# Retention units of 256 tokens and 4 heads in 512-byte rows on 64 by 64 tiles, with the whole program in a searched order

## The chip, the cores and the metric

One core of one Trainium2 chip. The metric is device microseconds of one execution. A change of less than 2% counts as the same. A run over 1.5% above the fastest of its kernel is called slow and left out of the ratios. In the kernel text, tiles in PSUM take the results of matmuls; `dma_start_transpose` (a DMA transpose) copies a tile and swaps its rows and columns on the way, which `nc.tensor.transpose` does on TensorE.

## The reference, cut to what matters

```python
batch, n_heads, seq, head_dim = (4, 8, 768, 64)          # float32 throughout
# part 1: retention, for every batch and head
for t in range(S):
    state = gamma * state + k[t] (x) v[t]                # 64 x 64 outer product
    x[t]  = scale * q[t] @ state
# part 2, for every batch, d_model = 512
theta = x @ w_theta
zr, zi = x * cos(theta), x * sin(theta)
y = w_tok_r @ zr + w_tok_i @ zi                          # 768 x 768, over tokens
u = x + y
out = u + relu(u @ w_ch)
```

## The kernel before

Tokens are cut into 24 chunks of 128 with all 8 heads. Decay is put into q and v by exponents (`qsc`, `vsc`), so a chunk is scores, outputs and a state sum. The parts that the change touches:

```python
def load_chunk(n):                       # q, k, v: 256 KB each, rows of 64 floats
    for name, src in (("kf", k), ("qf", q), ("vf", v)):
        t = io.tile([P, H, D], FT, name=name, bufs=9)
        nc.sync.dma_start(out=t, in_=src[b, :, c * P:(c + 1) * P, :].rearrange("h s d -> s h d"))
...
N_DMA = (B - 1) * nT + 1                 # chunks from here on: k, q and x transposed by DMA
M_DMA = (B - 2) * nT                     # output tiles from here on: u transposed by DMA
...
def att_A(n):                            # scores: 4 x 2 matmuls, 64 rows by 128 columns
    for j in range(NP):
        for par in range(2):
            rows = slice(par * D, (par + 1) * D)
            nc.tensor.matmul(at_ps[:, par, j, :], kqT[rows, j, :], kqT[rows, NP + j, :], ...)
...
def att_Y(n):                            # outputs, then the state sum, which stays in PSUM
    ...
    for j in range(NP):
        nc.tensor.matmul(st_ps[b][:, j, :], s["kb"][:, j * P:(j + 1) * P],
                         s["vb"][:, j * P:(j + 1) * P], start=(c == 0 and j == 0), ...)
...
for s_ in range(last_slot):              # the order: one loop over slots
    if n is not None and n + 5 < NCH and n >= nT + 2:
        load_chunk(n + 5)
    ...
```

All loads, stores and DMA transposes stand on one queue, SyncE's, in program order. With `N_DMA` = 19 and `M_DMA` = 12 the DMA transposes (5 of k and q, 5 of x, 11 of u) come when the loads are nearly done. GpSimd makes all bf16 copies of k, q and v; VectorE makes all products z.

Of the kernel before, what the change touches and what calls it, by code (L numbers as in the profile page):

```python
# [14 lines left out]
FT = mybir.dt.float32  # L15
# [3 lines left out]
PSUM = bass.MemoryType.PSUM  # L19

# [12 lines left out]
def kernel(  # L33
# [13 lines left out]




# [6 lines left out]
    NP = H // 2  # L57
    scale = 1.0 / math.sqrt(D)
    gammas = [1.0 - 2.0 ** (-5.0 - h) for h in range(H)]
    NCH = B * nT  # L60

    N_DMA = (B - 1) * nT + 1
    M_DMA = (B - 2) * nT
# [8 lines left out]


    raw = {}

    def load_chunk(n):
        b, c = divmod(n, nT)
        for name, src in (("kf", k), ("qf", q), ("vf", v)):
            t = io.tile([P, H, D], FT, name=name, bufs=9)
            nc.sync.dma_start(  # L80
                out=t, in_=src[b, :, c * P:(c + 1) * P, :].rearrange("h s d -> s h d"))
            raw[n, name] = t

    wdma = {}

    def load_w512(name, src):
        t = io.tile([P, nD, dm], FT, name="w512", bufs=2)
        nc.sync.dma_start(out=t, in_=src.rearrange("(a p) e -> p a e", p=P))
        wdma[name] = t

    def load_wtok(r, t0):
        src = (moe_w_tok_r, moe_w_tok_i)[r]
        t = io.tile([P, S], FT, name="wtok", bufs=4)
        nc.sync.dma_start(out=t, in_=src[t0 * P:(t0 + 1) * P, :])  # L94
        wdma[r, t0] = t

    for what in ("c0 c1 th c2 c3 c4 w0 c5 w1 w2 c6 w3 c7 ch c8 w4 c9 c10 w5 c11 "
                 "c12").split():
        if what == "th":
            load_w512("th", moe_w_theta)  # L100
        elif what == "ch":
            load_w512("ch", moe_w_ch)
        elif what[0] == "c":
            load_chunk(int(what[1:]))
        else:
            for r in range(2):
                load_wtok(r, int(what[1:]))


    posn = const.tile([P, nT], FT)  # L110
    nc.gpsimd.iota(posn, pattern=[[P, nT]], base=1, channel_multiplier=1,
                   allow_small_or_imprecise_dtypes=True)
    lg = const.tile([P, H], FT)
    for h in range(H):
        nc.gpsimd.memset(lg[:, h:h + 1], math.log(gammas[h]))
    lscale = const.tile([P, 1], FT)
    nc.gpsimd.memset(lscale, math.log(scale))
    halfpi = const.tile([P, 1], FT)
    nc.gpsimd.memset(halfpi, math.pi / 2.0)
    zerob = const.tile([P, 1], FT)  # L120
    nc.gpsimd.memset(zerob, 0.0)
    arg = const.tile([P, nT, H], FT)
    nc.vector.tensor_mul(arg, _bcast_last(posn, H), _bcast_mid(lg, nT))
    vsc = const.tile([P, nT, H], FT)
    nc.scalar.activation(vsc, arg, AF.Exp, bias=zerob, scale=-1.0)
    qsc = const.tile([P, nT, H], FT)
    nc.scalar.activation(qsc, arg, AF.Exp, bias=lscale, scale=1.0)
    ident = const.tile([P, P], BF)
    make_identity(nc, ident)
    mask = const.tile([P, P], BF)  # L130
    nc.gpsimd.memset(mask, 1.0)
    nc.gpsimd.affine_select(out=mask, in_=mask, compare_op=ALU.is_ge, fill=0.0,
                            base=0, pattern=[[1, P]], channel_multiplier=-1)
    stbd = []
    for i in range(2):
        t = const.tile([P, NP, P], BF, name=f"stbd{i}")
        nc.vector.memset(t, 0.0)
        stbd.append(t)

    wth = const.tile([P, nD, dm], BF)  # L140
    wch = const.tile([P, nD, dm], BF)
    wT = [const.tile([P, nT, S], BF, name="wtr"), const.tile([P, nT, S], BF, name="wti")]
# [4 lines left out]
    def att_prep(n):  # L147
        c = n % nT
        r3 = "p (h d) -> p h d"
        kqb = work.tile([P, 2, dm], BF, name="kqb", bufs=5)  # L150
        kb, qb = kqb[:, 0, :], kqb[:, 1, :]
        vb = work.tile([P, dm], BF, name="vb", bufs=5)
        nc.gpsimd.tensor_copy(kb.rearrange(r3, h=H), raw[n, "kf"])  # L153
        nc.gpsimd.tensor_mul(qb.rearrange(r3, h=H), raw[n, "qf"],  # L154
                             _bcast_last(qsc[:, c], D))
        nc.gpsimd.tensor_mul(vb.rearrange(r3, h=H), raw[n, "vf"],  # L156
                             _bcast_last(vsc[:, c], D))
        st[n] = dict(kqb=kqb, kb=kb, qb=qb, vb=vb)

    def att_T(n):  # L160
        s = st[n]
        kq_ps = psum.tile([P, 2 * NP, P], BF, name="kq_ps", tag="tr", bufs=2)
        for i, src in enumerate((s["kb"], s["qb"])):
            for j in range(NP):
                nc.tensor.transpose(kq_ps[:, i * NP + j, :],  # L165
                                    src[:, j * P:(j + 1) * P], ident)
        kqT = work.tile([P, 2 * NP, P], BF, name="kqT", bufs=4)
        nc.vector.tensor_copy(kqT, kq_ps)  # L168
        s["kqT"] = kqT

    def att_T_dma(n):
        s = st[n]
        kqT = work.tile([P, 2 * NP, P], BF, name="kqT", bufs=4)
        nc.sync.dma_start_transpose(
            out=kqT, in_=s["kqb"].rearrange("p a d -> p (a d)"))
        s["kqT"] = kqT

    def att_A(n):
        s = st[n]
        kqT = s["kqT"]  # L180
        at_ps = psum.tile([P, 2, NP, P], FT, name="at_ps", tag="at", bufs=1)
        for j in range(NP):
            for par in range(2):
                rows = slice(par * D, (par + 1) * D)
                nc.tensor.matmul(at_ps[:, par, j, :], kqT[rows, j, :],  # L185
                                 kqT[rows, NP + j, :], start=(j == 0),
                                 stop=(j == NP - 1), skip_group_check=True)
        at = work.tile([P, 2, NP, P], BF, name="at", bufs=2)
        nc.vector.tensor_mul(at.rearrange("p a j t -> p (a j) t"),  # L189
                             at_ps.rearrange("p a j t -> p (a j) t"),  # L190
                             _bcast_mid(mask, H))
        s["at"] = at

    st_ps = {}
    xs, zs = {}, {}

    def att_Yinter(n):
        c = n % nT
        s = st[n]
        s["yT_ps"] = psum.tile([P, NP, P], FT, name="yT_ps", tag="acc", bufs=2)  # L200
        if c > 0:
            for j in range(NP):
                nc.tensor.matmul(s["yT_ps"][:, j, :], stbd[c % 2][:, j, :],  # L203
                                 s["kqT"][:, NP + j, :], start=(j == 0), stop=False,
                                 skip_group_check=True)

    def att_Y(n):
        b, c = divmod(n, nT)
        s = st[n]
        yT_ps = s["yT_ps"]  # L210
        for j in range(NP):
            for par in range(2):
                h = 2 * j + par
                nc.tensor.matmul(yT_ps[par * D:(par + 1) * D, j, :],  # L214
                                 s["vb"][:, h * D:(h + 1) * D], s["at"][:, par, j, :],
                                 start=(c == 0 and j == 0), stop=(j == NP - 1),
                                 skip_group_check=True)
        if c < nT - 1:
            if c == 0:
                st_ps[b] = psum.tile([P, NP, P], FT, name="st_ps", tag="st", bufs=1)  # L220
            for j in range(NP):
                nc.tensor.matmul(st_ps[b][:, j, :], s["kb"][:, j * P:(j + 1) * P],  # L222
                                 s["vb"][:, j * P:(j + 1) * P],
                                 start=(c == 0 and j == 0),
                                 stop=(c == nT - 2 and j == NP - 1),
                                 skip_group_check=True)
        if c == 0:
            xs[b] = big.tile([P, nT, dm], BF, name="x_sb")
            zs[b] = big.tile([P, nT, 2, dm], BF, name="z")
        xT = work.tile([P, NP, P], BF, name="xT", bufs=3)  # L230
        nc.scalar.copy(xT, yT_ps)  # L231
        s["xT"] = xT
        if c < nT - 1:
            for par in range(2):
                sl = slice(par * D, (par + 1) * D)
                nc.scalar.copy(stbd[(c + 1) % 2][sl, :, sl], st_ps[b][sl, :, sl])  # L236

    def att_X_dma(n):
        b, c = divmod(n, nT)
        nc.sync.dma_start_transpose(  # L240
            out=xs[b][:, c, :].rearrange("p (j e) -> p j e", j=NP),
            in_=st[n]["xT"].rearrange("p j t -> p (j t)"))

    def att_X(n):
        b, c = divmod(n, nT)
        s = st[n]
        if n < N_DMA:
            x_ps = psum.tile([P, NP, P], BF, name="x_ps", tag="tr", bufs=2)
            for j in range(NP):
                nc.tensor.transpose(x_ps[:, j, :], s["xT"][:, j, :], ident)  # L250
# [267 lines left out]
```

## Time and profile before

| | before |
|---|---|
| time, median of the first 3 runs | 185.08 us (183.41 to 185.79) |
| profiled span | 181.8 us, granted clock 0.994 |
| TensorE idle in all (trace) | 20.2 us |
| DMA transposes | 21 |
| time from 60 to 118 us below 100 GB/s | 1.2 us |

The page's lines on the engines, the packets and the chain of waits:

```profile
PE 157.7 (87%) x1367; PEld 90.7 (50%) x1392; DVE 104.8 (58%) x146; ACT 74.7 (41%) x140; POOL 79.9 (44%) x104
DMA packets 95265, 35.63 MB, mean 196 GB/s; under 512 B 89488, under 2 KB 89744, under 8 KB 95248
PE 62%; SPq 18%; DMA 12%; issue 2%; POOL 2%; DVE 1%; DVEq 0%
```

The reader is to see that TensorE makes up 62% of the chain that ended last, that nearly all packets are under 512 bytes, and that VectorE has a lot of room (58%).

### The profile page before, as it was taken

How to read it: one execution, taken by the hardware profiler on the slowest of the kernel's cores; microseconds unless marked ns; L12 is line 12 of the kernel's file. 1: busy time of each engine (PE TensorE's matmuls, PEld its weight loads, DVE VectorE, ACT ScalarE, POOL GpSimd, SP SyncE). 2: the span in 40 equal slices, each digit the busy share in tenths (PEclk: the TensorE clock that was granted, in tenths of full speed). 3: DMA queues.
4: the chain of work that ended last, by engine and by line, in shares of the span. 5: the costliest groups of instructions: out<-in, count | busy, mean ns of one | idle time of the engine just before them, and what ended most of it. 6: DMA issues, size and time to landing. Idle time of an engine off the chain costs nothing.

```text
span 181.8 us, 3528 instructions
## 1 busy us (share of the span) xinstructions
PE 157.7 (87%) x1367; PEld 90.7 (50%) x1392; DVE 104.8 (58%) x146; ACT 74.7 (41%) x140; POOL 79.9 (44%) x104
## 2 busy tenths in 40 slices
PE   0567987897764999999999999999999999999991
PEld 0344655553542655656565565455545544444560
DVE  1264794716822777878676877765645744434442
ACT  4053764821429535647554363356345332200010
POOL 4648677869075768865777847250000000000000
PEclk9999999999999999999999999999999999999997
DMA  6999999999998999999999989984483333334433
GB/s 128 222 316 218 224 276 259 294 288 231 227 259 180 260 243 225 222 272 271 223 228 251 266 208 233 263 151 115 119 112 102 103 97 90 104 93 110 132 105 117
DMA packets 95265, 35.63 MB, mean 196 GB/s; under 512 B 89488, under 2 KB 89744, under 8 KB 95248
## 3 DMA queue, kind: packets, MB, share of 16 engines
q1 hardware_dynamic: 95104, 35.27, 86.4%
q8 instruction: 11, 0.18, 0.5%
q10 hardware_dynamic: 144, 0.13, 0.2%
q14 instruction: 6, 0.05, 0.1%
HBM read 25.69 MB, written 6.29 MB: 176 GB/s over the span
## 4 chain that ended last, share of the span: by engine, by line
PE 62%; SPq 18%; DMA 12%; issue 2%; POOL 2%; DVE 1%; DVEq 0%
PE y_ps L282 27%; SPq L80 15%; PE o_ps L310 11%; PE th_ps L253 8%; DMA kf<-in_k_dram 4%; DMA qf<-in_q_dram 3%; PE yT_ps L214 3%; DMA wtok<-in_moe_w_tok_r_dram 3%; PE at_ps L185 3%; PE kq_ps L165 3%; PE st_ps L222 2%; SPq L94 2%; DMA uT<-u 2%; PE yT_ps L203 2%; PE x_ps L250 1%
## 5 line engine op out<-in xcount | busy, mean ns | idle before, releaser
L282 PE MATMUL y_ps<-z,wti 128*128 128x512 bf16 x137 | 51.9, 379 | 1.6 <-ACT wti L332 0.9
L282 PE MATMUL y_ps<-z,wtr 128*128 128x512 bf16 x125 | 47.4, 379 | 0.7 <-DVE u L287 0.3
L189 DVE TENSOR_TENSOR at<-at_ps,mask 128x1024 bf16<-128x1024 f32 x24 | 29.3, 1220 | 8.9 <-PE at_ps L185 8.8
L258 ACT ACTIVATE cs<-th_ps,halfpi 128x512 bf16<-128x512 f32 x24 | 16.5, 688 | 38.0 <-PE th_ps L253 34.1
L154 POOL TENSOR_TENSOR kqb<-qf,qsc 128x512 bf16<-128x512 f32 x24 | 25.7, 1071 | 11.3 <-DMA qf<-in_q_dram 11.1
L156 POOL TENSOR_TENSOR vb<-vf,vsc 128x512 bf16<-128x512 f32 x24 | 25.9, 1081 | 7.0 <-DMA vf<-in_v_dram 5.8
L264 DVE TENSOR_TENSOR z<-cs,x_sb 128x1024 bf16<-128x1024 bf16 x24 | 19.6, 818 | 14.2 <-ACT cs L259 14.2
L168 DVE COPY kqT<-kq_ps 128x1024 bf16<-128x1024 bf16 x19 | 13.1, 691 | 24.6 <-PE kq_ps L165 24.4
L253 PE MATMUL th_ps<-wth,xT 128*128 128x512 bf16 x89 | 24.4, 387 | 2.4 <-DVE wth L395 1.9
L153 POOL CAST kqb<-kf 128x512 bf16<-128x512 f32 x24 | 16.0, 667 | 19.9 <-DMA kf<-in_k_dram 14.1
L310 PE MATMUL o_ps<-wch,uT 128*128 128x512 bf16 x88 | 23.1, 379 | 0.4 <-DMA uT<-u 0.2
L165 PE MATMUL kq_ps<-ident,kqb 128*128 128x128 bf16 x152 | 13.6, 234 | 11.1 <-POOL kqb L153 7.0
L287 DVE TENSOR_TENSOR u<-y_ps,x_sb 128x512 bf16<-128x512 f32 x23 | 15.8, 690 | 11.9 <-PE y_ps L282 11.9
L313 DVE SCALAR_TENSOR_TENSOR ot<-o_ps,u 128x512 f32<-128x512 f32 x23 | 15.9, 692 | 10.7 <-PE o_ps L310 10.7
L231 ACT CAST xT<-yT_ps 128x512 bf16<-128x512 f32 x24 | 14.1, 586 | 19.4 <-PE yT_ps L214 18.1
L282 PEld LDWEIGHTS <-wti 128*128 128x128 bf16 x138 | 13.5, 98 | 15.4 <-issue 1.9
L282 PEld LDWEIGHTS <-wtr 128*128 128x128 bf16 x138 | 13.5, 98 | 13.5
L165 PEld LDWEIGHTS <-kqb 128*128 128x128 bf16 x152 | 10.6, 104 | 16.5 <-POOL kqb L153 7.9
L259 ACT ACTIVATE cs<-th_ps,zerob 128x512 bf16<-128x512 f32 x24 | 16.3, 681 | 0.0
L236 ACT CAST stbd<-st_ps 64x256 bf16<-64x256 f32 x40 | 14.7, 366 | 0.5
L310 PEld LDWEIGHTS <-uT 128*128 128x128 bf16 x92 | 8.8, 98 | 10.3 <-DMA uT<-u 0.4
L253 PEld LDWEIGHTS <-xT 128*128 128x128 bf16 x96 | 8.8, 100 | 9.2 <-issue 2.6
(51 smaller groups left out, 147.3 us busy)
## 6 DMA issues: line engine op xcount, KB each, us to landing
kf<-in_k_dram SPq DMA_DIRECT2D x24, 256.0 KB, 4.9
qf<-in_q_dram SPq DMA_DIRECT2D x24, 256.0 KB, 5.0
vf<-in_v_dram SPq DMA_DIRECT2D x24, 256.0 KB, 5.3
out_dram<-ot SPq DMA_DIRECT2D x23, 256.0 KB, 2.2
wtok<-in_moe_w_tok_r_dram SPq DMA_DIRECT2D x6, 384.0 KB, 5.3
wtok<-in_moe_w_tok_i_dram SPq DMA_DIRECT2D x6, 384.0 KB, 5.9
w<-in_moe_w_theta_dram SPq DMA_DIRECT2D x1, 1024.0 KB, 6.7
w<-in_moe_w_ch_dram SPq DMA_DIRECT2D x1, 1024.0 KB, 7.8
```

Of the source, the lines that this page charges most:

```text
L80: nc.sync.dma_start(out=t, in_=src[b, :, c * P:(c + 1) * P, :].rearrange("h s d -> s h d"))
L153: nc.gpsimd.tensor_copy(kb.rearrange(r3, h=H), raw[n, "kf"])
L154: nc.gpsimd.tensor_mul(qb.rearrange(r3, h=H), raw[n, "qf"], _bcast_last(qsc[:, c], D))
L156: nc.gpsimd.tensor_mul(vb.rearrange(r3, h=H), raw[n, "vf"], _bcast_last(vsc[:, c], D))
L165: nc.tensor.transpose(kq_ps[:, i * NP + j, :], src[:, j * P:(j + 1) * P], ident)
L189: nc.vector.tensor_mul(at.rearrange("p a j t -> p (a j) t"), at_ps.rearrange("p a j t -> p (a j) t"), _bcast_mid(mask, H))
L253: nc.tensor.matmul(th_ps, s["xT"][:, j, :], wth[:, j, :], start=(j == 0), stop=(j == NP - 1))
L258: nc.scalar.activation(cs[:, 0, :], th_ps, AF.Sin, bias=halfpi, scale=1.0)
L259: nc.scalar.activation(cs[:, 1, :], th_ps, AF.Sin, bias=zerob, scale=1.0)
L264: nc.vector.tensor_mul(zs[b][:, c], st[n]["cs"], _bcast_mid(xs[b][:, c, :], 2))
L282: nc.tensor.matmul(y_ps, wT[r][:, s0, t0 * P:(t0 + 1) * P], zs[b][:, s0, r, :], start=(s0 == 0 and r == 0), stop=(s0 == nT - 1 and r == 1))
L310: nc.tensor.matmul(o_ps, mo[m]["uT"][:, j, :], wch[:, j, :], start=(j == 0), stop=(j == nD - 1))
```

## The change

Its intent: make the loads cheaper (rows of two tokens, 512 bytes), pack the small attention matmuls as 64 by 64 tiles, make one visit to the attention shapes per unit instead of three, and put every instruction where a search found it best. The core of the diff:

```diff
+ORDER = """
+Lk.0 Lq.0 Lv.0 Lk.1 const1 const2 Lq.1 const4 const6 Lth const3 const5 Lv.1 ck.0.p warm.8 Tk.0
+... (852 tokens in all: operation, unit or tile, engine; D* is a DMA transpose, T* one on TensorE)
+M.7.1 M.7.2 SU.13 XA.12.1 Dk.16 M.7.3 z.10.v SB.13.0.a SB.13.1.p Du.5 I.13 G.14 z.11.v M.7.4
+...
-    def load_chunk(n):
-        ...
-                out=t, in_=src[b, :, c * P:(c + 1) * P, :].rearrange("h s d -> s h d"))
+    def load_unit(name, src, n):
+        b, i, h = unit(n)                       # 256 tokens, 4 heads
+        t = io.tile([P, HU, 2, D], FT, name=name, bufs=9)
+        nc.sync.dma_start(
+            out=t.rearrange("p h a d -> p h (a d)"),
+            in_=src[b, h * HU:(h + 1) * HU, i * 2 * P:(i + 1) * 2 * P, :].rearrange(
+                "h (p a) d -> p h (a d)", a=2))
 ...
+    def A(n):                                   # 16 matmuls of 64 x 64 x 128; Y(n), ST(n) alike
+                        nc.tensor.matmul(at_ps[cols, g, j, a, :],
+                                         kqT[rows, 0, a, j, cols], kqT[rows, 1, :, j, cols], ...)
 ...
+    def SU(n):                                  # state sums: float32 in SBUF, added by VectorE
+            nc.vector.tensor_add(s2[i % 2][:, 1], ds[0], s2[i % 2][:, 0])
+        if i < nI - 1:
+            nc.vector.tensor_add(s2[(i + 1) % 2][:, 0], ds[1], s2[i % 2][:, 1])
 ...
+    def z(C, e):                                # the engine is given by the order:
+        engines[e].tensor_mul(st["z", b][:, c], st["cs", C], _bcast_mid(x_of(C), 2))
```

DMA transposes rise from 21 to 49.

## The prediction

> **What bounds the kernel now.** I read the page's slices first, then the sums by stretch, the DMA rates of the first stretch, the chain of waits, and a few microseconds of the timeline at full density. The slices show two regimes:
>
> ```profile
> PE   0567987897764999999999999999999999999991
> DMA  6999999999998999999999989984483333334433
> ```
>
> DMA is full for the first 26 slices (118 us); TensorE is full only from slice 13 (59 us) on. By stretch (TensorE, weight load, VectorE, ScalarE, GpSimd, granted clock, DMA share and GB/s):
>
> ```profile
> 0.00:59.00 59.00, 40.50 (x415) 25.16 (x422) 29.79 (x42) 27.02 (x50) 37.66 (x60) 1.00 1.06 240
> 59.00:118.00 59.00, 57.96 (x563) 34.94 (x573) 44.21 (x60) 29.38 (x56) 39.65 (x42) 1.00 1.13 244
> 118.00:172.00 54.00, 53.63 (x354) 26.82 (x360) 27.21 (x38) 17.52 (x34) 2.62 (x3) 1.00 0.47 109
> ```
>
> So the first 59 us are set by loads, the next 59 by TensorE with DMA just as full, the last 64 by TensorE alone. The chain of waits agrees: before 59 us it is nearly all queue issue and landings, after it nearly all matmuls.
>
> ```profile
> 42.13 7.52 DMA kf<-in_k_dram
> ...
> 51.51 6.18 DMA qf<-in_q_dram
> ...
> 83.46 0.33 PE at_ps L185 x8
> 83.79 0.34 PE yT_ps L214 x8
> 84.13 0.33 PE st_ps L222 x4
> ```
>
> How fast do loads go? The DMA rates of 2 to 20 us, in 40 slices:
>
> ```profile
> GB/s 108 239 282 275 245 205 227 224 222 214 212 223 222 219 220 245 245 382 382 391 396 370 286 274 221 217 217 218 218 214 218 220 216 218 218 219 218 216 219 217
> ```
>
> The right half is q, k and v alone, in rows of 64 floats (256 bytes): 218 GB/s, flat, 1.20 us per 256 KB load. The hump of about 385 is the theta weight, in 2048-byte rows. The row length sets the rate.
>
> What does TensorE cost when it is full? One chunk (start, duration; a matmul's duration includes its drain, so I take differences of starts):
>
> ```profile
> 82.86 0.38 PE L282 MATMUL y_ps<-z,wtr 128*128 128x512 bf16 x1
> 83.08 0.38 PE L282 MATMUL y_ps<-z,wti 128*128 128x512 bf16 x1
> 83.39 0.40 PE L185 MATMUL at_ps<-kqT 64*128 64x128 bf16 x8
> 83.72 0.41 PE L214 MATMUL yT_ps<-at,vb 128*64 128x128 bf16 x8
> 84.06 0.40 PE L222 MATMUL st_ps<-vb,kqb 128*128 128x128 bf16 x4
> 84.30 0.39 PE L250 MATMUL x_ps<-ident,xT 128*128 128x128 bf16 x4
> 84.52 1.03 PE L253 MATMUL th_ps<-wth,xT 128*128 128x512 bf16 x4
> ```
>
> A 512-column matmul takes 0.216 us. Four of 128 columns take 0.22 (x_ps). The attention trio takes 84.30 - (83.08 + 0.216) = 1.00 us, of which 0.66 is columns and about 0.1 at each of three changes of tile shape.
>
> **What the Trainium skill says.** "DMA: Bandwidth & Descriptors", sections Specifications and "Why small descriptors are slow (HBM only)", puts line rate at 512 bytes and up and gives 256-byte descriptors 11 cycles where 8 move data. The trace agrees on the direction (218 against 385 GB/s); nothing here has run at 512. "TensorEngine Tiling (Array Packing)", Key Properties, says changing the tiling mode drains TensorE while tiles of one mode run independently; the trace agrees (the 0.1 us before at_ps; eight 128-column matmuls of half size in the 0.22 that four whole ones take). Its Restrictions say column tiling turns off fast weight load; yT_ps, column tiled already, still keeps the pace. "SBUF — State Buffer", Who interferes with whom, says VectorE and GpSimd lock a shared port; z took 0.70 us usually and 1.34 beside GpSimd work at 25 us, which agrees.
>
> **The change part by part.** (1) Loads. 72 loads of 256 KB keep their bytes but use 512-byte rows. Per engine and packet, 256 bytes at 218 GB/s is 18.8 ns and 2048 at 385 is 85 ns; a straight line gives 28.3 ns for 512, so 290 GB/s and 0.90 us a load (estimate). Saved: 72 x 0.30 = 21.6 us of DMA time.
>
> (2) More transposes go to DMA: 17 of k and q against 5 (1024 packets of 256 bytes each, 1.2 us), 14 of x and 18 of u against 5 and 11 (0.6 us each): 39.6 against 15.6 us, adding 24.0. So the DMA total does not fall: before 72 x 1.20 + 15.6 + theta and channel weights 5.4 + token rows 12 x 0.98 + stores 24 x 0.68 = 135 us; after 65 + 40 + 5 + 12 + 16 = 138.
>
> (3) TensorE. Before: 480 matmuls of 512 columns, 103.7; trio 24 x 1.00 less four missing state sums, 23; k and q transposes 19 x 0.45 = 8.5; x 19 x 0.22 = 4.3; inter-chunk 20 x 0.22 = 4.5; u 2.9; token weights 4.0. Sum 151. After: the big ones as they are, 103.7; k and q 7 x 0.45 = 3.1; x 10 x 0.22 = 2.2; u 1.3; token weights 4.0; inter-chunk 16 x 0.22 + 8 x 0.11 = 4.4. The trio becomes one visit of 48 matmuls on 64 by 64 tiles, four at once: scores and outputs four rounds of 0.055 each, 0.22 + 0.22, state sums (64 columns) 0.11 to 0.22, and two changes of shape for three, 0.2: 0.75 to 0.87, take 0.8, x 24 = 19. Sum 138. Saved: 13 us.
>
> (4) State. The sum leaves PSUM for a float32 copy in SBUF: 40 small VectorE adds and 48 half-block casts on three engines. I put VectorE at 115 to 120 us for 105, GpSimd and ScalarE at 70 to 80. None bounds. PSUM pays: the transpose and accumulator pools lose their second buffer, and one y buffer must be read (0.69) before the next product starts, which the order fills with other matmuls.
>
> (5) Order. The end of a program in which DMA is full early and TensorE full late is at least (DMA time up to some transfer) + (TensorE work from its user on). Going through the order, the transfers that give the most sit late. One of them is the transpose of u of tile 11: ahead of it and with it on the one queue are 66 loads 59.7, the two wide weights 5.4, 12 token rows 11.8, 14 k/q transposes 16.8, 14 x and u transposes 8.4, 8 stores 5.4: 107.5 us. First bytes move at 2 us and a transpose lands 1.8 after its packets: 111. From its product on: 62 pairs of y matmuls 26.8, 14 outputs 12.1, 6 theta 5.2, 5 visits 4.0, 5 inter-chunk 1.1, the halved last tile 3.7: 53. Before, the last matmul ended 3.8 us ahead of the span's end. 111 + 53 + 4 = 168 with a DMA that never idles. Early transfers give less: the first six units (18 loads 16.3, theta 2.7) leave about 125 behind them, so about 150. TensorE alone gives 138 + 10 of start + 4 = 152.
>
> **Sum.** Span 168 by the DMA path, 2 to 4 more for DMA idling at waits of the queue, less what a 512-byte packet may be better than my line: 165 as the span. Timed runs stand 3.3 us over the profiled span now (185.1 and 181.8), so 168 as the time. The gain of 17 us is mostly TensorE time taken away (13) and an earlier start; DMA stays full to about 120 us.
>
> **The rivals.** (a) 512 bytes is nearly line rate: 0.75 us a load, 10 us less ahead of tile 11. For it: the skill's threshold; against it: 2048 bytes still cost a fixed part per packet. The time would be 159 to 162, with TensorE the bound again. (b) Small tiles do not run four at once (weights, or issue of 96 instructions in 0.6 us): a visit takes 1.4 instead of 0.8, 14 us more TensorE work, though part lies under full DMA. Against it: pairs start together in both directions now. Time 175 to 182. (c) The queue is the bound: a transpose holds it 1.2 us when idle and 2 to 4 when loaded; 49 of them with waits on VectorE and TensorE ahead of loads. For it: first-stretch pieces in which the queue waits for GpSimd. Time 173 to 178. (d) Single PSUM buffers stall TensorE 0.5 us a tile, 24 times: 12 us, mostly hidden under DMA up to 110 us, 4 or 5 after. Time 172.
>
> **Range and chances.** (a) pulls to 160, (b) to (d) to 178; each alone is a minor chance, and to stay within 2% (above 181.4) two of the bad ones must come together. Predicted 168, range 160 to 178. Faster 0.93, same 0.05, slower 0.02.
>
> **What would show it.** Load landings 0.90 us apart and 285 to 295 GB/s in the opening; TensorE lost time before it fills falling from 26 us (59 less the 33 of the 151 done by then) to about 20, spread rather than at the start; DMA full to about 115 us; visits of 0.75 to 0.87 us start to start; TensorE waits named on kqT, uT or x_sb from DMA. I am wrong if visits exceed 1.0 us, if loads come at 1.1 us or more, or if TensorE waits mostly for VectorE or ScalarE.

## The result, and the profile after

| | before | after |
|---|---|---|
| time, median of 4 runs | 184.25 us (182.23 to 185.79) | 190.99 us (189.85 to 191.56) |
| profiled span, granted clock | 181.8 us, 0.994 | 188.1 us, 0.937 |
| TensorE idle in all | 20.2 us | 32.0 us |
| below 100 GB/s, 60 to 118 us | 1.2 us | 13.8 us |

The ratio is 1.041, with an interval of 1.035 to 1.048: slower. All ratios in this text are the mean time of one kernel's fast runs over that of the other's fast runs of the same rounds, so not quite the ratio of the medians. Two of the four of before (185.08 and 185.79) are over 1.5% above its fastest; in the later rounds its medians were 182.9 to 183.5 us.

The lines that answer those of before:

```profile
PE 152.9 (81%) x1903; PEld 83.3 (44%) x1928; DVE 126.3 (67%) x205; ACT 68.0 (36%) x138; POOL 75.4 (40%) x100
DMA packets 79781, 40.94 MB, mean 218 GB/s; under 512 B 37136, under 2 KB 74256, under 8 KB 79760
PE 37%; DMA 30%; SPq 17%; DVE 7%; issue 3%; POOL 2%; ACT 2%; DVEq 0%; POOLq 0%; ACTq 0%
```

TensorE has less work, so that part of the change worked; its smaller share of the chain says only that other things are now waited for. DMA has gone from 12% to 30% of the chain with fewer packets, and VectorE from 1% to 7%. The slices of after (compare those in the prediction):

```profile
PE   7426967586999469999997859958988999999992
DMA  5999999999999999699968987798898750443563
GB/s 154 299 312 294 327 345 285 216 391 209 367 299 209 184 313 226 137 256 299 239 120 201 285 177 167 225 199 195 239 237 197 169 132 12 113 129 66 148 218 112
```

A slice is 4.7 us. Up to slice 12 the rates are 285 to 390 GB/s in many slices; from slice 13 to the end of the loads they are some 220 in the mean, though the busy digit is 7 to 9 in all of these but the two holes of 137 and 120, where it is 6. Queue busy and queue fast are two things. By the stretches of the prediction, the last here to 178 us (columns as there: TensorE, weight load, VectorE, ScalarE, GpSimd, clock, DMA share, GB/s):

```profile
0.00:59.00 59.00, 42.13 (x661) 25.55 (x667) 47.01 (x80) 28.02 (x54) 36.10 (x61) 0.88 1.09 285
59.00:118.00 59.00, 49.79 (x657) 26.72 (x666) 41.12 (x64) 21.46 (x46) 28.75 (x28) 0.91 1.00 219
118.00:178.00 60.00, 54.88 (x544) 26.95 (x552) 34.24 (x55) 17.74 (x37) 10.55 (x11) 1.00 0.68 159
```

In the first stretch DMA moves 285 GB/s against 240. In the second, where before had TensorE at 57.96 of 59 us, after has 49.79, at 219 GB/s against 244 and with a DMA share of 1.00. The loss is in the middle. Which waits make it? The chain of waits of after around 101 to 129 us (start, length, what):

```profile
101.23 3.09 DMA vf<-in_v_dram
104.32 5.89 DMA uT<-u
110.26 1.61 PE o_ps L494 x4
...
124.62 3.80 DMA x_sb<-xT
128.51 2.07 DVE z L434
```

A transpose of u takes 5.89 us from issue to landing at 104 us, though it has half the bytes of a load; the median of all its transposes of u is 2.6 us. Its packets show a part of why. A 256-byte packet of a transpose normally takes 18 ns. From 108.1 to 109.6 us 18 of them (and 9 of 4 bytes) stand for over 300 ns each and are then released within 0.04 us of one another; meanwhile next to nothing is moved. I call this a stuck group. Counting groups of at least four such packets, after has 14, of which 7 fall between 60 and 118 us; before has 3, all after 118 us. The group is not all of the 5.89 us: in a_copy_b below, where no packet is stuck, the plain copy of the same tile takes 5.49 us among the loads. The landings of uT, first of after, then of a_copy_b:

```profile
DMA to landing us min/median/max: 2.4/2.6/5.9
```

```profile
DMA to landing us min/median/max: 2.3/3.3/5.5
```

The second kind of loss is on VectorE. The timeline of after from 60.5 us (start, length; weight loads, ScalarE and the queue left out):

```profile
60.50 0.38 PE L467 MATMUL y_ps<-z,wti 128*128 128x512 bf16 x1
60.81 0.42 PE L309 MATMUL at_ps<-kqT 64*64 64x128 bf16 x16
60.94 4.64 POOL L434 TENSOR_TENSOR z<-cs,x_sb 128x1024 bf16<-128x1024 bf16 x2
61.05 0.39 PE L372 MATMUL r_ps<-at,vb 64*64 64x128 bf16 x16
61.28 0.29 PE L333 MATMUL ds_ps<-vb,kqb 64*64 64x64 bf16 x16
61.30 2.30 DVE L271 TENSOR_TENSOR vb<-vf,vsc 128x512 bf16<-128x512 f32 x1 [1.23 <-DMA vf<-in_v_dram]
...
63.53 2.33 DVE L135 CAST kqb<-kf 128x512 bf16<-128x512 f32 x1
...
65.78 1.21 DVE L318 TENSOR_TENSOR at<-at_ps,mask 128x1024 bf16<-128x1024 f32 x1
...
67.30 0.29 DVE L346 TENSOR_TENSOR s<-ds_ps,s 128x128 f32<-128x128 f32 x1
...
67.64 0.58 PE L479 MATMUL u_ps<-ident,u 128*128 128x128 bf16 x4 [4.24 <-DVE s L346]
```

Two products z on GpSimd run from 60.94 to 65.58. Beside them VectorE's two casts take 2.30 and 2.33 us; the means of these forms on VectorE are 0.91 and 0.86. TensorE needs the PSUM bank that VectorE's state sum reads, and stands 4.24 us. The three attention lines also show the packed visit: the three starts are 0.24 and 0.23 us apart, and from the end of the columns of y (60.50 + 0.22) to those of ds_ps (61.57) is 0.85 us. How dear z is on GpSimd stands in the page's groups (the busy us and the mean ns):

```profile
L434 POOL TENSOR_TENSOR z<-cs,x_sb 128x1024 bf16<-128x1024 bf16 x9 | 19.8, 2210 | 12.2 <-DMA x_sb<-xT 7.4
```

In the kernel before all 24 were on VectorE at 0.82 us in the mean.

### The profile page after: what moved, and what is told of

Same layout as the page of the kernel before. It is cut to its first block, busy times and chain, and to the rows that moved or that the text cites. A ratio compares the mean times of both kernels' runs of the same rounds, so it can differ in the third digit from the quotient of the medians.

```text
span 188.1 us, 4720 instructions
## 1 busy us (share of the span) xinstructions
PE 152.9 (81%) x1903; PEld 83.3 (44%) x1928; DVE 126.3 (67%) x205; ACT 68.0 (36%) x138; POOL 75.4 (40%) x100
## 4 chain that ended last, share of the span: by engine, by line
PE 37%; DMA 30%; SPq 17%; DVE 7%; issue 3%; POOL 2%; ACT 2%; DVEq 0%; POOLq 0%; ACTq 0%
PE y_ps L467 17%; SPq L148 11%; PE o_ps L494 8%; DMA vf<-in_v_dram 7%; DMA uT<-u 6%; DMA qf<-in_q_dram 6%; DMA w<-in_moe_w_ch_dram 5%; PE th_ps L420 5%; DMA kf<-in_k_dram 2%; SPq L176 2%; DMA x_sb<-xT 2%; ACT cs L427 2%; SPq L295 2%; PE at_ps L309 1%; PE y_ps L517 1%
## 5 line engine op out<-in xcount | busy, mean ns | idle before, releaser
L467 PE MATMUL y_ps<-z,wtr 128*128 128x512 bf16 x133 | 52.0, 391 | 2.9 <-DVE z L434 2.1
L392 ACT CAST xT<-r_ps 128x256 bf16<-128x256 f32 x48 | 15.7, 376 | 44.2 <-PE r_ps L372 44.2
L434 POOL TENSOR_TENSOR z<-cs,x_sb 128x1024 bf16<-128x1024 bf16 x9 | 19.8, 2210 | 12.2 <-DMA x_sb<-xT 7.4
L500 DVE SCALAR_TENSOR_TENSOR ot<-o_ps,u 128x512 f32<-128x512 f32 x23 | 15.8, 685 | 10.5 <-PE o_ps L494 10.3
L271 POOL TENSOR_TENSOR vb<-vf,vsc 128x512 bf16<-128x512 f32 x13 | 13.9, 1067 | 20.9 <-DMA vf<-in_v_dram 20.8
L467 PEld LDWEIGHTS <-wti 128*128 128x128 bf16 x138 | 13.8, 100 | 16.9 <-issue 4.2
L467 PEld LDWEIGHTS <-wtr 128*128 128x128 bf16 x138 | 13.8, 100 | 14.9 <-issue 1.4
L265 POOL TENSOR_TENSOR kqb<-qf,qsc 128x512 bf16<-128x512 f32 x15 | 15.8, 1051 | 11.4 <-DMA qf<-in_q_dram 11.3
L427 ACT ACTIVATE cs<-th_ps,zerob 128x512 bf16<-128x512 f32 x24 | 16.4, 687 | 10.8 <-PE th_ps L420 10.7
L434 DVE TENSOR_TENSOR z<-cs,x_sb 128x1024 bf16<-128x1024 bf16 x15 | 15.1, 1013 | 4.8 <-DMA x_sb<-xT 3.3
L135 POOL CAST sbd<-s 64x256 bf16<-64x256 f32 (+1 forms) x18 | 8.0, 446 | 23.7 <-DVE s L344 20.7
L359 PE MATMUL r_ps<-kqT,sbd 128*128 128x128 bf16 x80 | 8.9, 228 | 8.6 <-DVE sbd L135 4.3
L271 DVE TENSOR_TENSOR vb<-vf,vsc 128x512 bf16<-128x512 f32 x11 | 10.0, 912 | 8.1 <-DMA vf<-in_v_dram 8.1
L359 PEld LDWEIGHTS <-sbd 128*128 128x128 bf16 x80 | 6.2, 101 | 14.9 <-POOL sbd L135 6.2
## 6 DMA issues: line engine op xcount, KB each, us to landing
w<-in_moe_w_ch_dram SPq DMA_DIRECT2D x1, 1024.0 KB, 10.3
```

The costliest lines, as they stand in the source:

```text
L265: engines[e].tensor_mul(in_blocks(kqb_of(n)[:, 1]), by_token(raw["qf", n]), _bcast_last(K["qsc"][:, i, :, h * HU:(h + 1) * HU], D))
L271: engines[e].tensor_mul(in_blocks(vb), by_token(raw["vf", n]), _bcast_last(K["vsc"][:, i, :, h * HU:(h + 1) * HU], D))
L392: nc.scalar.copy(st["xT", 2 * i + c][:, 2 * h:2 * h + 2].rearrange("p j (t a) -> p j t a", a=2), st["R", n][:, c, :2 * P].rearrange("p (j ...
L427: nc.scalar.activation(st["cs", C][:, w, :], st["th_ps", C], AF.Sin, bias=K["zerob" if w else "halfpi"], scale=1.0)
L434: engines[e].tensor_mul(st["z", b][:, c], st["cs", C], _bcast_mid(x_of(C), 2))
L467: nc.tensor.matmul(st["y", t], K["wT"][r][:, s0, t0 * P:(t0 + 1) * P], st["z", b][:, s0, r, :], start=(s0 == 0 and r == 0), stop=(s0 == nT ...
```

## The experiments

Theory A: transposes by DMA among the loads stall the DMA engines, or hold queue and users, far beyond their packets. Theory B: the z on GpSimd lock VectorE, which holds TensorE. Rivals: the rows are no better than before; the packed matmuls are slow; the queue's instruction order alone is at fault; the lower clock is at fault. Eighteen kernels ran. "Load phase" is the time with loads on the queue: the last load is issued at 114.8 us in before and at 138.6 us in after. Ratios are to the kernel before in the same rounds.

### First set: transposes away, or more of them

**a_copy**: all 49 DMA transposes become plain DMA copies of the same bytes in 256-byte rows (padded tiles keep the rows apart; the sine's argument is multiplied by 0); wrong results.

```diff
-        nc.sync.dma_start_transpose(out=st["uT", t], in_=st["u", t])
+        nc.sync.dma_start(out=st["uT", t], in_=st["u", t].rearrange("p (j e) -> p j e", j=nD))
```

> The changed kernel with its 49 DMA transposes replaced by plain SBUF-to-SBUF copies of the same bytes in the same 256-byte rows, at the same places of the queue (results wrong on purpose; Sin gets scale 0 to stay in its range). Theory A, a DMA transpose among loads stalls all the DMA engines: the 18 us between 60 and 140 us in which less than 100 GB/s moves shrink to under 5, and the time falls from 191 to 170-177. Theory B, it is only that 256-byte packets fill the DMA engines: 188-191. Theory C, the fixed order makes the engines wait for loads whatever the transposes do: 186-191.

Measured 177.89 us, ratio 0.968 (0.960 to 0.977), no stuck group at all, TensorE idle 21.1 us (in the profiled run, a slow one). The time is just above the 170 to 177 of theory A, and the slow DMA time from 60 to 140 us went from 17.9 to 10.2 us, not under 5; the kernel before has 12.7 there, since its loads end early. So 13 us hang on the transposition itself, not on the bytes, the rows or the places in the queue. Transposition includes how long an instruction holds the queue: in the medians 1.2 us for a transpose of x or u and 1.5 for one of k and q, and 0.6 for each of their copies in a_copy_b. The trace's granted clock read 0.949 over most of it, since the wrong values were huge; a_copy_b below repairs that.

**a_pe_all**: all 49 on TensorE, with evictions on VectorE (k, q) and ScalarE (x, u). Correct.

```diff
-Dk.n   -Dx.n   -Du.n
+Tk.n Tq.n E.n   +Tx.n Ex.n.a   +Tu.n Eu.n.a
```

> The changed kernel with all 49 DMA transposes done by TensorE (k and q evacuated by VectorE, x and u by ScalarE), each at the first place where the PSUM bank is free. TensorE's dense work rises from 138 to 153 us, DMA falls from 138 to 98. Theory A and B: DMA no longer sets the middle, 173-180. Theory C: the waits for loads stay and 15 us of TensorE work and more bank contention come on top, 195-205.

Measured 204.6 us, ratio 1.118. TensorE becomes the bound:

```profile
PE 167.4 (82%) x2165; PEld 98.4 (48%) x2192; DVE 136.2 (67%) x222; ACT 87.0 (43%) x170; POOL 74.2 (37%) x100
```

Its busy time rises by 14.5 us and the 49 transposes share one PSUM bank that an eviction must free each time (five waits of x_ps for ScalarE's eviction come to 2.9 us). The remedy costs more than the disease. The time lies in the range that was expected of theory C (195 to 205), not in that of A (173 to 180); as TensorE's own work rose so much, it does not decide between them.

**b_more**: the kernel before with as many DMA transposes as after, 49.

```diff
-    N_DMA = (B - 1) * nT + 1
-    M_DMA = (B - 2) * nT
+    N_DMA = nT + 2
+    M_DMA = nT
```

> The kernel before with this part of the change alone: DMA transposes from chunk 8 on (16 of k/q and 16 of x for 5 and 5, 18 of u for 11 or 12). TensorE loses 11 x 0.67 + 6 x 0.22 = 9 us, DMA gains 23 us of packets. Theory A: slower than before by 4% or more, 191-205, with stalls of the DMA engines as in the changed kernel. Theory B: DMA is full to 140 instead of 118 us, 186-192. Theory C: the TensorE work saved shows, 176-184.

Measured 209.84 us, ratio 1.145, above even the 191 to 205 of theory A. 6 of its 9 stuck groups fall in 60 to 118 us, but the test is spoilt: the first transposes stand behind the loads of the opening list, and TensorE waits 20.2 us once for a kqT. That is the order of the queue.

```profile
PE at_ps L185 <- DMA kqT<-kqb: 23.2, 4, 20.2
```

**a_rows256**: the changed kernel with each load as two, which were meant to have 256-byte rows.

```diff
-            out=t.rearrange("p h a d -> p h (a d)"), in_=... "h (p a) d -> p h (a d)"
+            for g in range(2):  out=t[:, 2 * g:2 * g + 2], in_=... "h (p a) d -> p h a d"
```

> The changed kernel with each load of q, k, v made of two loads in 256-byte rows, as before the change (bytes the same, twice the packets). If DMA is what bounds the changed kernel (A and B): 72 x (1.20 - 0.84) = 26 us more DMA, 208-217. Theory C: the order hides part, 193-203.

Measured 206.87 us, ratio 1.128. But the edit did not do what was meant. Its packets (compare the line of after above):

```profile
DMA packets 80933, 40.95 MB, mean 200 GB/s; under 512 B 38288, under 2 KB 75408, under 8 KB 80912
```

With 256-byte rows there would be 73,728 more packets under 512 bytes. There are 1,152 more, all of 4 bytes, and 36,864 of 512 bytes as in after: a pair of tokens stayed one row. What the edit changed is the number of load instructions, 144 of 128 KB for 72 of 256 KB, and that alone cost 16 us, so the expected ranges do not apply; in the medians a half load holds the queue 0.47 us, a whole one 0.57. What the rows are worth in the time no run tests. That they are better the trace of after shows: a 512-byte packet takes 27 ns in the median, one of 256 bytes in before 18. So the rival "the rows are no better" falls. The rates of its opening from 12 to 16 us, in 40 slices:

```profile
GB/s 292 292 292 287 292 287 287 307 277 297 287 292 287 297 287 287 297 287 277 302 297 282 292 297 287 282 297 282 302 277 297 292 287 297 282 287 435 292 271 271
```

Flat at 292 GB/s, where before had 218.

### Second set: values, queue, partial moves

**a_copy_b**: a_copy with the decay exponents set to zero, so that values stay ordinary.

```diff
-                                 bias=bias, scale=sc)
+                                 bias=bias, scale=0.0 * sc)
```

> The changed kernel with plain copies for DMA transposes again, now also with the decay exponents set to zero, so that the wrong values stay of ordinary size (in the first such run they grew by many orders, and the granted clock read 0.95 for 100 us). Theory A (stalls of the DMA engines by transposes cost the middle 13 to 18 us): no packet of 256 bytes stuck, TensorE without a wait over 1 us from 30 us on except the one at 64 us, clock 1.0 in the middle, 169-175. If the lower clock had nothing to do with the values: 176-179 again. Theory C: over 185.

Measured 178.54 us, ratio 0.980 (0.973 to 0.987), clock 1.0 through the middle. The low clock of a_copy came from its values and hardly mattered. The expected 169 to 175 was missed: something besides the transposes costs time. The lower clock of after (0.937) is not it either: a_zdve_u below took 178.9 us at the same 0.937, and a_xp_u took 181.7 us at 1.0 and 179.3 at 0.959.

**a_actq**: all DMA transposes issued from ScalarE's queue.

```diff
-        nc.sync.dma_start_transpose(
+        nc.scalar.dma_start_transpose(
```

> The changed kernel with all 49 DMA transposes issued from ScalarE's queue, loads and stores left alone on SyncE's. If the harm is that a transpose holds the loads' queue (1.2 us of issue, and waits for its producer with loads behind it): the dry spells of the DMA engines go, 180-186. If the harm is in the DMA engines themselves, stuck 256-byte packets released together stay (8 or more groups between 60 and 140 us), and 188-198, since ScalarE also gets 59 us of issue.

Measured 210.37 us, ratio 1.150. There are still 14 stuck groups, so the groups are not a matter of SyncE's queue order. The time is above both ranges (180 to 186, 188 to 198), for another reason: ScalarE's own work now waits behind its transposes, and TensorE behind ScalarE:

```profile
PE r_ps L359 <- ACT cs L427: 18.8, 6, 7.4
```

So this run does not tell what the holding of SyncE's queue costs.

**a_hyb1**: the 24 transposes of k, q, x and u of the load phase on TensorE, the late ones by DMA. **a_pe_xu**: all x and u on TensorE, k and q by DMA. Their edits are those of a_pe_all, for fewer tokens.

> The changed kernel with the DMA transposes of the load phase (k/q of units below 18, x of chunks below 16, u of tiles below 12: 11, 6 and 7 of them) done by TensorE, the late ones left to DMA. TensorE dense work rises by 8 us to 146. Theory A: no stalls among loads, 177-186. Theory B: the same direction, since 256-byte packets fall by 21 us of DMA: 180-188. Theory C: 195-205 as with all of them on TensorE (204.6).

> The changed kernel with x and u transposed by TensorE (7 us more of it) and k/q still by DMA: separates the 17 large from the 32 small DMA transposes. If each transpose among loads costs a stall, a third of the stalls stay and the time is 185-192; if the kernel is bound by its fixed order, 193-200.

Measured 191.66 us (ratio 1.048) and, in a single run of unknown state, 193.78 us. The first is outside all three ranges. a_hyb1 has no stuck group from 60 to 118 us and yet gains nothing: TensorE's busy time is 160.4 us for 152.9, and its slices stand mostly at 7 and 8 until the loads end. Its slow DMA time from 60 to 118 us is even 29.8 us (32.3 in a_pe_all), 25.9 of them with fewer than three packets under way: the queue waits for results, 10.3 us at once for a store. a_pe_xu keeps 6 groups in that time, from k and q. Moving the work wholesale swaps one bound for another.

### Third set: GpSimd's z

**a_zdve**: the nine z of GpSimd on VectorE. **a_copy_zdve**: this and a_copy_b together; wrong.

```diff
-z.1.p   -z.5.p   -z.6.p   ... (9)
+z.1.v   +z.5.v   +z.6.v   ... (9)
```

> The changed kernel with the nine z products of GpSimd (2.2 us each) given to VectorE (0.7 each), nothing else. Theory E, GpSimd's long z locks VectorE out of SBUF (VectorE instructions of up to 3.0 us there, TensorE's 4.2 us wait at 64 us and 7 us of half clock after it): VectorE's time above each form's shortest falls from 15 to under 9 us, the wait at 64 us goes, 182-187. If only the DMA transposes matter: 189-193.

> Both suspects taken away: plain copies in place of the DMA transposes (values of ordinary size, wrong) and all z on VectorE. If the two causes make up what the prediction missed: 168-174. If z on GpSimd costs nothing once the stalls are gone: 177-180.

a_zdve measured 186.25 us, ratio 1.014 (1.005 to 1.023): VectorE gets nine more products, and the kernel gets 4.7 us faster. The wait at 64 us shrinks from 4.24 to 0.87 us:

```profile
64.53 0.38 PE L477 MATMUL u_ps<-ident,u 128*128 128x128 bf16 x4 [0.87 <-DVE s L344]
```

VectorE's time above the shortest of each form falls from 15.5 to 9.0 us, and the mean of its cast of k from 0.86 to 0.42. That is theory B. That a z is simply done sooner on VectorE is no rival: no wait of TensorE for a z of GpSimd is in the list of after. The stuck groups stay (12, of which 6 from 60 to 118 us). a_copy_zdve measured 175.53 us, ratio 0.958 (0.950 to 0.965). It misses the 168 to 174 expected if A and B were all that the prediction had overlooked. The two theories add up nearly: 191.0 to 178.5 for A alone, to 186.3 for B alone, to 175.5 for both (medians of different rounds, in which the kernel before lay between 183.0 and 184.3). The DMA rates from 60 to 140 us, first of after, then of a_copy_zdve (40 slices of 2 us, then the packets of that window):

```profile
GB/s 223 259 143 335 292 293 254 79 139 175 294 172 364 266 298 226 233 194 76 73 237 260 275 300 106 260 135 158 173 268 209 240 202 193 197 159 266 210 303 162
DMA packets 42053, 17.40 MB, mean 218 GB/s; under 512 B 22656, under 2 KB 40764, under 8 KB 42044
```

```profile
GB/s 265 276 309 285 298 315 197 294 218 293 318 253 280 262 253 154 255 286 292 283 267 194 272 252 268 345 231 234 253 271 277 291 171 174 241 324 82 194 11 66
DMA packets 46790, 19.60 MB, mean 245 GB/s; under 512 B 26963, under 2 KB 44988, under 8 KB 46780
```

The values of after under 150 (143, 79, 139, 76, 73, 106, 135) have none to match them, until the loads run out at the right end. Time below 100 GB/s from 60 to 118 us: after 13.8, a_zdve 11.6, a_copy_b 4.1, a_copy_zdve 2.7 us. So transposes account for 8.9 to 9.7 us of slow DMA, and for 10.7 to 12.5 us of the time. GpSimd's z account for 3.0 to 4.7 us of it.

**a_eng**: z on VectorE, all casts of k, q and v from unit 2 on GpSimd, state blocks on ScalarE. **a_eng_hyb**: this, with the transposes of a_hyb1 on TensorE.

```diff
-z.n.p  -ck.n.v  -cv.n.v  -SB.n.g.p ...
+z.n.v  +ck.n.p  +cv.n.p  +SB.n.g.a ...
```

> The changed kernel with the engines dealt as in the kernel before: from unit 2 on all casts of k, q, v on GpSimd, z on VectorE, the state blocks on ScalarE; order and transposes as changed. Theory E with A: VectorE's share falls, transposes still stall: 179-187. Rival: GpSimd's 2.75 us a unit, against 2.5 us for its loads, becomes the bound of the load stage: 189-195.

> As the last, and the DMA transposes of the load phase (11 of k/q, 6 of x, 7 of u) on TensorE. If both causes act and PSUM's single transpose bank costs little: 176-183, under the kernel before. If the bank is what made the all-TensorE version 204.6: 186-192, as without the dealing of engines (191.7).

Measured 187.02 us (1.019) and 190.6 us (1.041). VectorE's busy time falls to 106 us and nothing is gained over a_zdve, so with z moved VectorE's amount of work is no bound. Again the wholesale move of transposes gives nothing; 190.6 lies in the range expected if PSUM's one bank for transposes is what costs (186 to 192).

### Fourth and fifth sets: small moves, and the converse in the kernel before

**b_kq13**: before, with k, q and x transposed by DMA from chunk 13 on.

```diff
-    N_DMA = (B - 1) * nT + 1
+    N_DMA = (B - 2) * nT + 1
```

> The kernel before with one number changed: k, q and x of chunks 13 to 18 are transposed by DMA instead of TensorE, so 12 more transposes stand among loads, and the loads that are in the opening list stay ahead of all of them (the flaw of the run b_more is avoided). TensorE loses about 4 us of work (6 x 0.45 + 6 x 0.22). Theory A (transposes among loads stall the DMA engines, about 0.4 us each): at least 5 new groups of stuck 256-byte packets before 118 us (only one such group is there in the kernel before), and the time goes up by 2 to 8 us, to 185 to 191. Rival (the stalls belong to the order or the row size of the changed kernel): no new groups, 179 to 183.5.

Measured 191.07 us, ratio 1.046 (1.039 to 1.052). Three stuck groups appear from 60 to 118 us, not the five expected, and slow DMA time there rises from 1.2 to 6.4 us. Of the 9.6 us by which TensorE's idle time grows, 7.6 are one wait:

```profile
PE at_ps L185 <- DMA kqT<-kqb: 11.5, 5, 7.6
```

That transpose was issued at 86.3 us, behind loads that ran late, and landed at 90.5. The time is just at the upper end of theory A's range. So the test supports A in direction, but most of its cost is a user that waits for a transpose in the queue, not a stuck group.

**b_u6**: before, with the u of tiles 6 to 11 by DMA too; their output products come one slot later and take another PSUM bank.

```diff
-    M_DMA = (B - 2) * nT
+    M_DMA = (B - 3) * nT
```

> The kernel before with one number changed: the u transposes of tiles 6 to 11 by DMA instead of TensorE, 6 more transposes among loads, TensorE 1.3 us less work, their output products one slot later. It mirrors a_zdve_u. Theory A (a transpose among loads costs some 0.4 us or more of DMA and holds the queue 1.2 to 2 us): 184.5 to 189, with new groups of stuck packets before 118 us. Rival (only the changed kernel's order makes them costly): 181.5 to 184.

Measured 186.69 us, ratio 1.024 (1.017 to 1.032), for six transposes. Only one stuck group falls before 118 us. What costs is the first landing: issued at 98.3, landed at 102.3 us, 3.9 us, where the late ones of the same kernel take 2.4.

```profile
PE o_ps L310 <- DMA uT<-u: 4.7, 1, 4.7
```

So the kernel before also pays for transposes among loads, about as much as was expected, by the landing for which TensorE waits more than by stuck groups.

**a_zdve_u**: a_zdve with the seven u transposes of tiles 5 to 11 on TensorE. **a_zdve_xp**: a_zdve with six pairs of x transposes in one DMA instruction each. **a_xp_u**: both. **a_xp_u_k**: both, and k and q of units 6 and 8 on TensorE. All are correct.

```diff
-Du.5 ... Du.11
+Tu.5 Eu.5.a ... Tu.11 Eu.11.a
+    def Dp(i):                                  # xT of tiles 2i and 2i+1 in one tile
+        nc.sync.dma_start_transpose(
+            out=st["x", b][:, c:c + 2].rearrange("p c (j e) -> p (c j) e", j=4),
+            in_=st["xTp", i].rearrange("p c j t -> p (c j t)"))
```

> The changed kernel with z on VectorE and the u transposes of tiles below 12 (7 of them, the ones with loads behind them) on TensorE. TensorE gains 7 x 0.22 = 1.5 us of work; 7 transposes leave the loads. If each of the 31 transposes among loads costs 11/31 = 0.35 us, the time is 186.3 - 2.5 + 1.5 or about 185; if u's are the ones that matter (o_ps waited 2.7 us on one), 181 to 184; if TensorE's PSUM bank costs more than that, 187 to 190.

> The changed kernel with z on VectorE (186.3 before this) and the x transposes of six pairs of tiles as one DMA instruction of twice the size each: 43 transposes instead of 49, the same packets. If a stall comes once an instruction, some 6 x 0.4 us of stalls go: 183 to 185. If it comes per packet or by chance of what is in flight: 185 to 188, as the pair also has to wait for its second half.

> The changed kernel with z on VectorE, six pairs of x transposes in one instruction each, and the u transposes of tiles below 12 on TensorE: the three edits that each gave 3 to 5 us, together. If their gains are of different stalls: 176 to 179, clearly below the kernel before (183.3). If they are of the same stalls (each shortens the same queue): 180 to 182.

> As a_xp_u, and the k and q transposes of units 6 and 8 on TensorE as well (0.9 us more TensorE work, two DMA transposes fewer before 60 us). If the queue is still what sets that stage: 1 to 2 us under a_xp_u. If TensorE and VectorE set it (VectorE has 17 to 18 of 20 us busy there and each move gives it one eviction more): 0 to 2 us over a_xp_u.

| kernel | median us | ratio | below 100 GB/s, 60 to 118 us | of it with stuck packets | stuck groups |
|---|---|---|---|---|---|
| a_zdve | 186.25 | 1.014 (1.005 to 1.023) | 11.6 us | 6.0 us | 6 |
| a_zdve_xp | 183.57 | 0.992 (0.985 to 0.999) | 10.7 us | 6.5 us | 7 |
| a_zdve_u | 181.09 | 0.992 (0.985 to 0.999) | 9.8 us | 6.4 us | 10 |
| a_xp_u | 180.60 | 0.989 (0.983 to 0.994) | 9.4 us | 8.6 us | 10 |
| a_xp_u_k | 179.88 | 0.986 (0.981 to 0.990) | 9.2 us | 8.8 us | 8 |

Two of the four runs of a_zdve_xp and of a_zdve_u and one each of a_zdve and a_xp_u were slow; they are in the medians. The slow ones of a_zdve_u had no lower clock than its fast ones (0.991 and 0.951 against 0.937 and 0.966), so its spread is wide and a difference of 1% between these kernels means little. Each small move gains 2% or so, and together they do not add up: a_xp_u lies in the range expected if they mend the same stalls. a_zdve_xp (183 to 185 expected) and a_zdve_u (181 to 184) came out at the lower end; the 0.7 us from a_xp_u to a_xp_u_k decide nothing. The best, a_xp_u_k, beats the kernel before by 1.4%, still within 2%. Fewer transposes did not make fewer stuck groups (42 transposes gave 10 from 60 to 118 us, 49 gave 6), so "one stall per transpose" is not the rule. What goes as the queue gets fewer transposes of x and u is the slow time without a stuck packet: 5.6 us in a_zdve, 4.2 and 3.4 with one of the two edits, 0.8 with both. (The fifth column counts the slow 0.1 us in which a packet of up to 256 bytes that takes over 300 ns is under way.) And a_zdve_u lost the longest wait for one: TensorE's matmuls waited 3.1 us for a uT at 103 us in a_zdve, and 0.7 at most in a_zdve_u (first a_zdve, then a_zdve_u):

```profile
PE o_ps L492 <- DMA uT<-u: 3.6, 2, 3.1
```

```profile
PE o_ps L493 <- DMA uT<-u: 0.7, 1, 0.7
```

## Why the prediction was wrong, step by step

**Step 1, loads: right.** Predicted 290 GB/s and 0.90 us a load; 292 GB/s measured. What that is worth in the time was not tested (a_rows256 did not change the rows). Rival (a), nearly line rate, did not come.

**Step 3, TensorE: right.** A visit was put at 0.75 to 0.87 us; 0.85 measured. Rival (b), tiles that do not run at once, did not come. The work of the matmul columns falls from 136.3 to 127.7 us in the records (0.216 us for 512 columns, a tile weighted by its share of the array, which is my count), 8.6 us; with the changes of shape, which the columns leave out, the prediction had said 13.

**Step 2, the transposes: the term that was mis-sized.** The prediction gave each k and q transpose 1.2 us and each x and u transpose 0.6 us of packets, and let them fill the queue like loads. The runs show a cost beyond the packets: with copies of the same bytes in the same places the kernel is 12.5 us faster (191.0 to 178.5), or 10.7 with z moved. A part of it is likely the one queue (argued from the traces, not shown by a run of its own), on which the prediction let loads and transposes follow one another at the pace of their packets. Up to the issue of the last load the queue is held by its own instructions for 120.7 of 138.6 us in after, and for 97.4 of 124.9 us in a_copy_b; the last load lands at 141.2 and 128.6 us, in the kernel before at 119.7.

**Step 4, "None bounds": wrong for VectorE in places.** Its 126.3 us were not far from the 115 to 120 predicted, and in the mean it has room. But the count of busy time left out what GpSimd's z does to the casts beside it. 4.7 us of time hang on that (191.0 to 186.3), 3.0 us with the copies in place (178.5 to 175.5).

**Step 5, the path: its form was right, "a DMA that never idles" was not.** The prediction said that the transposed u of tile 11 lands at 111 us and that 53 + 4 us follow. The same landing in the traces:

| kernel | uT of tile 11 lands | from there to the end of the span |
|---|---|---|
| predicted | 111 | 57 |
| after | 128.9 | 59.2 |
| a_zdve (z moved) | 124.0 | 59.2 |
| a_copy_b (copies) | 118.5 | 58.3 |
| a_copy_zdve (both) | 116.0 | 58.8 |

The remainder held to some 2 us in every variant. The landing came 18 us late: 12.9 of these go with the two causes, and 5 stay. The path had allowed for a first byte at 2 us and then for no waiting at all; what the 5 us are, no run here tells. A small slip besides: the 3.3 us between timed runs and profile compared a median with the profile of the fastest run (183.41 against a span of 181.8); run by run the difference is 1.6 to 1.9 us.

**The earlier start** that the prediction counted on did not come: by 59 us the matmuls on record in after add up to 28.3 us of columns (without 8 on zeros that only warm TensorE up), those of before to 29.1, by the same count as above.

**Rival (c), the queue as the bound,** was the nearest to what happened. It had the cause (transposes that hold the queue for longer than their bytes) with too small a size: 173 to 178 for the 191 that came. a_rows256, by its accident, shows the same from another side: 72 more instructions on the queue, with the same packets of data, cost 16 us. The sign "TensorE waits named on kqT, uT or x_sb from DMA" came true, and so did, in places, one of the signs of being wrong: the 4.24 us for which TensorE waits on VectorE.

**What stays open.** Why the packets of a transpose get stuck and come free together: the trace does not name the DMA engines of packets. Six of the 14 groups of after come free within 3.2 us of the start of a 16 KB instruction fetch, too few to call a cause. How the 12.5 us split between stuck groups and the time for which a transpose holds the queue is not settled either. Of the 13.8 us of slow DMA time in after, 5.9 us fall in time with stuck packets, so less than half; and the small moves got faster while that part grew from 6.0 to 8.6 us, which speaks for the queue. Longer landings are not what transposes add in after, as those of the copies are no shorter (median 3.3 us against 2.6 for u). A test would be a transpose that holds the queue no longer than a copy; none was run.

## What to carry to other kernels

A DMA transpose among loads is not priced by its bytes: price it by how long it holds the queue and by what a landing takes there, and keep the ones with near users off the queue (here seven of 49 moved to TensorE gave 2%, all of them lost 7%). Count the instructions on a queue too: twice as many loads of half the size cost 16 us here. And look at the packets of a test kernel before you believe what its edit says. When one path is a sum of transfers, check the rate in GB/s and not the busy share, because a queue can be busy and stuck. When work is moved to GpSimd, look at what VectorE does beside it.

## What the Trainium skill lacked or had wrong

- "Advanced Engine Details and Errata", X-Bar Transpose (TRN2), says that transpose DMAs are as fast as regular DMAs. Among loads they are not here: plain copies of the same bytes in the same places were 12.5 us faster (a_copy_b), and 7 groups of stuck packets from 60 to 118 us went to none; a transpose of u also holds the queue 1.2 us, its copy 0.6.
- "DMA: Bandwidth & Descriptors" gives 512 bytes as the least for line rate but no trn2 rate for such rows. Here they ran at 292 GB/s, against 218 for 256 bytes and 385 for 2048, so 512 bytes were short of the rate of longer rows.
- "TensorE: Matmul & The Clock Gate", Why this matters for your kernels, warns of gaps over about 3 us. Here a gap of 2.69 us (107.57 to 110.26 in after) was already followed by 3.4 us at half clock from 110.6, and one of 2.23 us at 123.7 was not.
